# First mixture in pairs of 512 tokens with a written instruction order; second layer of five experts with stationary weights and sums transposed back

## The chip, the cores and the metric

The kernel runs on one core of a Trainium2 chip. The metric is the device time of one launch in microseconds (us), as the median of several runs. TensorE does matmuls and transposes, VectorE, ScalarE and GpSimd do element-wise work, SyncE (SP) issues most DMAs. Instructions of one engine run in the order in which they were issued to it and wait for other engines by semaphores. SBUF is the on-chip memory, PSUM the small memory (eight banks of 128 x 512 fp32) into which TensorE writes.

## The reference

Three layers follow each other: a decayed linear attention over 1536 tokens (2 x 768) of width 512, a first mixture with a cosine as its nonlinearity, and a second mixture in which every token goes to the one of eight experts with the largest gate.

```python
# attention in blocks of 64, with a decayed state; its output is x [1536, 512]
h = x @ w_in                    # [1536, 2048]
x = (h * np.cos(h)) @ w_out     # [1536, 512]

logits = x @ w_gate             # [1536, 8]
e_idx = np.argmax(logits, axis=1)
gate_w = probs[np.arange(N), e_idx]
eom = 1.0 / (1.0 + np.exp(-(x @ w_output_gate)))
for e in range(8):
    mask = e_idx == e
    h = np.maximum(x[mask] @ w1[e], 0.0)            # [., 1024]
    out[mask] = gate_w[mask, None] * eom[mask, e, None] * (h @ w2[e])
```

## The kernel before

All large products are made of three matmuls on fp32 values that are split into a high part (rounded to the fp32r format) and a low part (the rest): high x high, high x low, low x high. `w_in` and `w_out` come as 64-bit floats and are put together from two 32-bit words ("words": a ScalarE operation, three on VectorE, then the high part on ScalarE and the low one on GpSimd). The experts' weights are fp32: the high part is a ScalarE cast (1024 columns, L769 or L203), the low one a VectorE subtraction (L776 or L204).

The tokens of the first mixture are in six blocks `j` of 256, its 2048 hidden columns in eight pieces `p` of 256. One step `("B", j, p)` does one piece for one block. `mm_l1` (L460) makes 24 matmuls with 128 x 128 weights stationary and 256 tokens moving (L467). `chain_parts` (L501) computes h*cos(h) in seven operations that alternate between ScalarE and VectorE (L507, L508, L509, L512, L513, L516, L517), over 512 columns: two halves of the piece by 256 tokens. `mm_l2` (L484) makes 12 matmuls with 128 tokens of the result stationary and 512 columns of `w_out` moving (L488). The second layer of a step is issued two steps behind its first layer (LAG), so that TensorE has other work while the chain runs. Two PSUM banks hold first-layer results; a bank is free when the chain's product (L513) has read it.

The order of steps: six steps (blocks 0 to 2, pieces 0 and 1) run beside the attention; then 24 steps, for each piece the blocks 3, 4 and 5; then 18 steps, blocks 0, 1 and 2 one after the other, pieces 2 to 7. Until the attention ends the instructions stand in an order written out by hand; the steps after it are put in order by a scheduler, with hints (`late`), and from the end of the first mixture on the order is written out again.

When a block is done, the router's pieces follow: `r_evac` adds up its rows, `r_tr` transposes them, `r_mm` multiplies with the gates, `r_arg` picks the expert, `r_rank` (L624) finds each token's place and scatters its row into a table in DRAM by an indirect DMA of GpSimd (L646). Blocks 3, 4 and 5 end first, then 0, 1 and 2. After block 0 the first 128 rows of experts 0 and 1 are read back (`h_rows`, L718) and transposed (`h_prep`, L725).

Experts 0 and 1 are done in two halves of 128 rows (`h_l1`, `h_turn`, `h_l2`), the first before all tokens are routed. Experts 2 to 7 take 208 rows each at once, in four quarters of the hidden columns. For one quarter `c_first` (L779) makes, for each half, four pairs of matmuls with 128 x 128 weights stationary and the tokens moving: 416 columns (high and low parts of the 208 tokens, L477) and 208 columns (L478), then adds the two column groups (L787, L788), applies the relu and splits again. `c_second` (L811) calls `mm_l2`: 12 matmuls with 104 tokens stationary and 512 output columns moving, into two PSUM banks (L488). After the fourth quarter `c_store` scales the rows and scatters them to the output (L699, L701, L702). PSUM is two banks for first layers and six for everything else.

Of the kernel before, what the change touches and what calls it, by code (L numbers as in the profile page):

```python
# [24 lines left out]
WIDE = 256.0  # L25
# [3 lines left out]
def kernel(  # L29
# [29 lines left out]
    EARLY = 0  # L59
# [19 lines left out]
    tmp_p = ctx.enter_context(tc.tile_pool(name="tmp", bufs=2))  # L79

# [50 lines left out]
    HP = 2  # L131
    steps = [("B", j, p) for j in range(FIRST) for p in range(HP)]
# [5 lines left out]
    order.sort(key=lambda z: min(i for i, y in enumerate(steps) if y[2] == z[1]) + 2 * (z[0] == "out"))  # L138
# [26 lines left out]
    nxt = {"load": 0, "split": 0, "free": 0}  # L165
    pools = {}

    def w_load():
# [8 lines left out]
        if not pools.get("spare") and nxt["free"] and i % 3 == 0:  # L177
            pool, tag = xt_p, "xt"
        if "raw2" in pools and i % 2:
            pool = pools["raw2"]  # L180
        t = pool.tile([128, 1024], I32 if words else F32, tag=tag, name="raw")
# [6 lines left out]
    def w_tile(a, p, name):  # L188
        pool = (wa_p if a else wb_p) if p < HP else pools["w2a" if a else "w2b"]
        return pool.tile([128, 2, 1024], F32R, tag=f"w{p}", name=name)  # L190

    half_done, high_done = [], []

    def split_words():
        i = nxt["split"]
        if i >= len(order):
            return
# [3 lines left out]
        if key[0] in ("w1", "w2"):  # L201
            t = w_tile(key[0] == "w1", place(*key), "w_" + "_".join(str(z) for z in key))
            nc.scalar.copy(out=t[:, 0, :], in_=r)  # L203
            nc.vector.tensor_sub(out=t[:, 1, :], in0=r, in1=t[:, 0, :].bitcast(F32))  # L204
            wt[key] = t
            return
        name, p, f = key
        if f == 0:
# [6 lines left out]
        nc.vector.tensor_scalar(x, x, 3, None, ALU.logical_shift_left)  # L215
        nc.vector.scalar_tensor_tensor(
            out=x, in0=low, scalar=29, in1=x, op0=ALU.logical_shift_right, op1=ALU.bitwise_or)
        nc.vector.scalar_tensor_tensor(
            out=x, in0=high, scalar=-0x80000000, in1=x, op0=ALU.bitwise_and, op1=ALU.bitwise_or)
# [6 lines left out]
        half_done.append((hi, lo, xf))  # L226
# [15 lines left out]

    def w_split():
        split_words()
        split_parts()
        w_load()
# [103 lines left out]
    def xs_tile(slot, name="xs"):  # L350
        return xs_p.tile([128, 2, KD, TB], F32R, tag=f"xs{slot}", name=name)
# [88 lines left out]

    def clear_rows():
# [31 lines left out]

    def mm_rows(key, x, f):
# [17 lines left out]
    heads, ends = [], []  # L492

    def late(i, fn):
        with ExitStack() as order:
            if 0 <= i < len(heads):
                for ins in heads[i]:
                    order.enter_context(tc.issue_after(ins))
            fn()

    def chain_parts(h):  # L501
# [3 lines left out]

        def whole():
            head = nc.scalar.activation(out=t, in_=h, func=AF.Identity, bias=quarter, scale=INV2PI / WIDE)  # L507
            heads.append((head.ins, nc.scalar.activation(out=a, in_=t, func=AF.Identity, bias=magic).ins))  # L508
            nc.vector.scalar_tensor_tensor(out=a, in0=a, scalar=MAGIC, in1=t, op0=ALU.subtract, op1=ALU.subtract)  # L509
# [5 lines left out]
        def parts():  # L515
            high = nc.scalar.copy(out=g[:, 0].rearrange("p f t -> p (f t)"), in_=a)  # L516
            low = nc.vector.tensor_sub(  # L517
                out=g[:, 1].rearrange("p f t -> p (f t)"), in0=a,
                in1=g[:, 0].rearrange("p f t -> p (f t)").bitcast(F32))
            ends.append((high.ins, low.ins))  # L520

        return g, whole, wave, parts

    def cos_chain(h):
        g, *fns = chain_parts(h)
        for fn in fns:
            fn()
        return g


# [22 lines left out]
    def r_evac(j, accs):  # L553
        if j == FIRST:
            xr = xs_tile(0, "xrow").bitcast(F32).rearrange("p s k n -> p (s k n)")[:, 0:2 * ROW].rearrange(
                "p (t n) -> p t n", t=2)
        else:
            xr = pools["xr"].tile([128, 2, ROW], F32, tag="xrow", name="xrow")
        if j in part:
            half = part.pop(j)  # L560
            nxt["free"] += 1
            for t in range(2):
                nc.vector.scalar_tensor_tensor(
                    out=xr[:, t, 0:DM], in0=accs[t], scalar=WIDE ** -2, in1=half[:, t * DM:(t + 1) * DM],
                    op0=ALU.mult, op1=ALU.add)
        else:
            nc.scalar.activation(out=xr[:, 0, 0:DM], in_=accs[0], func=AF.Copy, scale=WIDE ** -2)
            nc.vector.tensor_scalar(xr[:, 1, 0:DM], accs[1], WIDE ** -2, None, ALU.mult)
# [3 lines left out]
        xrow_t[j] = xr  # L572

    def r_tr(j, tiles=(0, 1)):
        xr = xrow_t[j]
        if "x2T" not in lps_t:
            lps_t["x2T"] = xs_p.tile([128, KD, TB], F32, tag="xs2", name="x2T")
        x2T = lps_t["x2T"]
        for t in tiles:
            ps = acc_tile([128, KD, 128], "x2ps")  # L580
            for kk in range(KD):
                nc.tensor.transpose(ps[:, kk, :], xr[:, t, kk * 128:(kk + 1) * 128], ident)
            nc.scalar.copy(out=x2T[:, :, t * 128:(t + 1) * 128], in_=ps)

    def r_mm(j):

        lps = acc_tile([128, 512], "lps")
        for kk in range(KD):
            o = 32 * kk % 128
            nc.tensor.matmul(  # L590
                lps[o:o + 32, 0:TB], lhsT=wgs[:, kk, :], rhs=lps_t["x2T"][:, kk, :],
                start=True, stop=True, skip_group_check=True)
        lt = tmp_p.tile([128, 512], F32, tag="t", name="lt")[:, 0:TB]
        nc.vector.tensor_copy(out=lt, in_=lps[:, 0:TB])
        lg_t[j] = lt
# [3 lines left out]
    def r_arg(j):  # L599
        xr = xrow_t[j]  # L600
        lt = lg_t.pop(j)
        ps = acc_tile([128, 512], "l2ps")
        for t in range(2):
            nc.tensor.transpose(ps[:, t * 128:(t + 1) * 128], lt[:, t * 128:(t + 1) * 128], ident)
        lg = xr[:, :, DM:DM + E]
        nc.vector.tensor_reduce(
            out=xr[:, :, DM:DM + 2 * E],
            in_=ps[:, 0:256].rearrange("p (t k e) -> p t e k", t=2, e=32)[:, :, 0:2 * E],
            op=ALU.add, axis=AX.X)
        mx = pools["rt"].tile([128, 2, 1], F32, tag="mx", name="mx")  # L610
        ex = expert[:, 2 * j:2 * j + 2].unsqueeze(2)
        oh = pools["rt"].tile([128, 2, E], F32, tag="oh", name="oh")
        ohb = pools["rt"].tile([128, 2, E], BF16, tag="ohb", name="ohb")
# [652 lines left out]
```

## Time and profile before

| | |
|---|---|
| median of three runs | 528.23 us (527.96 to 528.28) |
| profiled execution, its own time | 529.07 us |
| its span (first to last instruction) | 527.3 us |
| TensorE busy, matmuls | 517.1 us, 98% of the span |
| VectorE, ScalarE, GpSimd busy | 348.2, 308.7, 93.9 us |
| attention with first steps, about | 0 to 100 us |
| first mixture up to its last second layer, about | to 342 us |
| experts 0 and 1, about | to 400 us |
| experts 2 to 7, about | to 521 us |

The durations of single instructions include their passage through the engine. TensorE starts the next matmul long before the end of the one before, so the distance between starts is what an instruction costs there. A row of the timeline gives the start of a group of like instructions, the time to the end of the last, and their number.

### The profile page before, as it was taken

The numbers are of one execution on the slowest core, as the hardware profiler recorded it, in microseconds if no ns is written. First come the engines' busy times: TensorE is split into PE (matmuls) and PEld (weight loads), VectorE is DVE, ScalarE is ACT, GpSimd is POOL, SyncE is SP. The second block draws the span as 40 slices with busy tenths as digits, with TensorE's granted clock in tenths as the row PEclk, the third lists the DMA queues.
The fourth block names the chain that finished last, engine by engine and source line by source line (L and its number), as shares of the span: only waits on it lengthen the run. The fifth ranks groups of instructions, "written<-read, shape, count | busy, mean of one in ns | idle before, by whom it ended". The sixth has DMA issues, their size and how long they took to land. (4 is left out here: it accounts for less than half of the span.)

```text
span 527.3 us, 9379 instructions
## 1 busy us (share of the span) xinstructions
PE 517.1 (98%) x3644; PEld 454.7 (86%) x3644; DVE 348.2 (66%) x652; ACT 308.7 (59%) x536; POOL 93.9 (18%) x129
## 2 busy tenths in 40 slices
PE   8989999999999999999999999999999999999995
PEld 7889988999899899888988898878888888888883
DVE  5887856887877864345466567753478787777731
ACT  3556655676686765554545566544577675766530
POOL 3364110332332320001021010211000101011011
PEclk9999999999999999999999999999999999999999
DMA  8999931346334383201252264726168878776301
GB/s 196 243 264 287 299 117 41 91 177 212 121 96 142 124 295 117 81 0 43 85 203 81 83 201 164 232 100 206 56 222 281 236 238 253 227 221 209 110 28 35
DMA packets 81939, 84.58 MB, mean 160 GB/s; under 512 B 41468, under 2 KB 61948, under 8 KB 81118
## 3 DMA queue, kind: packets, MB, share of 16 engines
q1 hardware_dynamic: 79646, 77.48, 48.5%
q0 software_dynamic: 2240, 6.42, 3.3%
q8 instruction: 30, 0.49, 0.4%
q14 instruction: 23, 0.19, 0.1%
HBM read 66.70 MB, written 17.65 MB: 160 GB/s over the span
## 5 line engine op out<-in xcount | busy, mean ns | idle before, releaser
L488 PE MATMUL acc<-w_out,g 128*128 128x512 f32 x576 | 140.9, 394 | 0.0
L488 PEld LDWEIGHTS acc<-w_out,g 128*128 128x128 f32 x576 | 105.0, 188 | 22.0 <-issue 1.4
L467 PEld LDWEIGHTS h<-xs,w_in 128*128 128x128 f32 x720 | 89.0, 191 | 2.1 <-DVE a L513 0.2
L467 PE MATMUL h<-xs,w_in 128*128 128x256 f32 x720 | 90.7, 283 | 0.0
L488 PE MATMUL acc<-w_w,g 128*104 128x512 f32 x288 | 70.6, 395 | 0.0
L509 DVE SCALAR_TENSOR_TENSOR a<-a,t 128x512 f32<-128x512 f32 x48 | 36.3, 755 | 46.5 <-ACT a L508 46.5
L776 DVE TENSOR_TENSOR w_w<-raw,w_w 128x1024 fp32r<-128x1024 f32 x50 | 60.6, 1216 | 0.8 <-ACT w_w L769 0.8
L488 PEld LDWEIGHTS acc<-w_w,g 128*104 128x104 f32 x288 | 46.7, 168 | 15.4
L477 PE MATMUL hw<-xs,w_w 128*128 128x416 f32 x192 | 59.0, 367 | 0.0
L467 PE MATMUL h<-xback,w_in 128*128 128x256 f32 x432 | 54.9, 283 | 0.0
L467 PEld LDWEIGHTS h<-xback,w_in 128*128 128x128 f32 x432 | 52.8, 189 | 1.4 <-issue 0.8
L507 ACT ACTIVATE t<-h,quarter 128x512 f32<-128x512 f32 x48 | 32.9, 685 | 34.3 <-PE h L467 34.2
L769 ACT CAST w_w<-raw 128x1024 fp32r<-128x1024 f32 x50 | 52.5, 1056 | 0.0
L478 PE MATMUL hw<-xs,w_w 128*128 128x208 f32 x192 | 49.3, 257 | 0.0
L516 ACT CAST g<-a 128x512 fp32r<-128x512 f32 x48 | 29.7, 620 | 32.0 <-DVE a L513 32.0
L513 DVE TENSOR_TENSOR a<-t,h 128x512 f32<-128x512 f32 x48 | 32.9, 685 | 19.6 <-ACT t L512 19.3
L512 ACT ACTIVATE t<-a 128x512 f32<-128x512 f32 x48 | 30.3, 632 | 25.0 <-DVE a L509 25.0
L702 POOL DMA_INDIRECT out_dram<-y,who x16 | 16.1, 1007 | 150.8 <-ACT y L699 147.4
L517 DVE TENSOR_TENSOR g<-a,g 128x512 fp32r<-128x512 f32 x48 | 33.1, 690 | 13.3 <-ACT g L516 12.6
L787 ACT COPY hsum<-hw 128x208 f32<-128x208 f32 x48 | 15.9, 332 | 38.5 <-PE hw L478 38.5
L478 PEld LDWEIGHTS hw<-xs,w_w 128*128 128x128 f32 x192 | 36.7, 191 | 1.0
L477 PEld LDWEIGHTS hw<-xs,w_w 128*128 128x128 f32 x192 | 36.1, 188 | 1.6
(148 smaller groups left out, 717.2 us busy)
## 6 DMA issues: line engine op xcount, KB each, us to landing
raw<-in_moe_w_dram SPq DMA_DIRECT2D x64, 512.0 KB, 4.4
raw<-in_moe_w_in_dram SPq DMA_DIRECT2D x16, 512.0 KB, 3.8
raw<-in_moe_w_out_dram SPq DMA_DIRECT2D x16, 512.0 KB, 3.5
xs_d<-zrow SPq DMA_DIRECT2D x16, 266.0 KB, 4.2
x_d<-xrow SPq DMA_DIRECT2D x6, 532.0 KB, 3.1
k<-in_k_dram SPq DMA_DIRECT2D x12, 256.0 KB, 5.6
q<-in_q_dram SPq DMA_DIRECT2D x12, 256.0 KB, 5.6
v<-in_v_dram SPq DMA_DIRECT2D x12, 256.0 KB, 5.3
```

Source lines behind the costliest of these rows:

```text
L467: nc.tensor.matmul(h[:, f * n:(f + 1) * n], lhsT=wA(key, ws, kk, f), rhs=x[:, xx, kk, :], start=(z == 0), stop=(z == 3 * KD - 1))
L477: nc.tensor.matmul(h, lhsT=wA(key, 0, kk, f), rhs=x[:, kk], start=(kk == 0), stop=False)
L478: nc.tensor.matmul(h[:, 0, :], lhsT=wA(key, 1, kk, f), rhs=x[:, kk, 0, :], start=False, stop=(kk == KD - 1))
L488: nc.tensor.matmul(accs[t][0:m], lhsT=g[:, gs, f, t * m:(t + 1) * m], rhs=wB(key, ws, f), start=(first and n == 0), stop=(last and n == 5))
L507: head = nc.scalar.activation(out=t, in_=h, func=AF.Identity, bias=quarter, scale=INV2PI / WIDE)
L509: nc.vector.scalar_tensor_tensor(out=a, in0=a, scalar=MAGIC, in1=t, op0=ALU.subtract, op1=ALU.subtract)
L512: nc.scalar.activation(out=t, in_=a, func=AF.Sin, scale=-TWOPI)
L513: nc.vector.tensor_mul(out=a, in0=t, in1=h)
L516: high = nc.scalar.copy(out=g[:, 0].rearrange("p f t -> p (f t)"), in_=a)
L517: low = nc.vector.tensor_sub(out=g[:, 1].rearrange("p f t -> p (f t)"), in0=a, in1=g[:, 0].rearrange("p f t -> p (f t)").bitcast(F32))
L769: nc.scalar.copy(out=t[:, 0, :], in_=r)
L776: nc.vector.tensor_sub(out=t[:, 1, :], in0=r, in1=t[:, 0, :].bitcast(F32))
```

## The change

*First mixture.* Blocks 3 and 4, and later blocks 0 and 1, are done in pairs of 512 tokens. A step `("P", j, (p, f))` does one half `f` of a piece for both blocks: 12 matmuls of the first layer with 512 tokens moving (`mm_duo`), the same chain over 512 columns, and 12 of the second layer for four groups of 128 tokens (`mm_duo2`). Blocks 5 and 2 (`SOLO` and the last) stay single. The number of steps stays 48; of the last 18, twelve are those of the pair 0 and 1, then six of block 2. The operands of a pair lie in one tile (`xs01`, `wa01`). Words are done one in each step; experts' weights from step `TURN` (30) on as they fall due (`turn_of`), one in a step, two in step `LATE` - 1 (41). The steps' instructions on TensorE, VectorE and ScalarE are written out in order: pieces of the chain, of a word, of a conversion, and the router's pieces, cut into a TensorE part and a vector part, in places given by `put(step, place, ...)`. PSUM is now two banks for first layers, four (`acc`) and two (`side`).

*Experts 2 to 6.* The second layer has `w2` stationary (128 x 128) and the tokens moving, again 416 and 208 columns, into four banks, one for each 128 output columns (`c_cols`). After the fourth quarter each bank's two column groups are added (a ScalarE copy and a VectorE addition), and at the third quarter of the next expert eight transposes bring the sums back to rows (`c_turn`), which `c_store` scales and scatters as before. Expert 7 is unchanged.

The core of the diff:

```diff
@@ steps, their order, and when pieces of the experts' weights are due
     steps = [("B", j, p) for j in range(FIRST) for p in range(HP)]
     NSA = len(steps)
-    steps += [("B", j, p) for p in range(NP) for j in range(FIRST, NB)]
-    steps += [("B", j, p) for j in range(FIRST) for p in range(HP, NP)]
+    for p in range(NP):
+        steps += [("P", FIRST, (p, f)) for f in range(2)] + [("B", SOLO, p)]
+    TURN = len(steps)
+    steps += [("P", 0, (p, f)) for p in range(HP, NP) for f in range(2)]
+    LATE = len(steps)
+    steps += [("B", FIRST - 1, p) for p in range(HP, NP)]
     NSB = len(steps)
...
         if at < HP:
-            return NSB - (FIRST - 1) * REST if w == "w2" else NSB - (FIRST - 1 - at) * REST
-        return NSB - (NP - at) + (2 if w == "w2" else 0)
+            return TURN + 2 + 5 * at if w == "w2" else LATE - 1
+        return NSB - (NP - at) + (3 if w == "w2" else 0)
@@ the pairs' matmuls
+    def mm_duo(key, x, f):
+        h = pools["l1"].tile([128, 2, TB], F32, tag="l1", name="h")
+        z = 0
+        for kk in range(KD):
+            for ws, xx in ((0, 0), (0, 1), (1, 0)):
+                nc.tensor.matmul(
+                    h, lhsT=wA(key, ws, kk, f), rhs=x[:, :, xx, kk, :], start=(z == 0), stop=(z == 3 * KD - 1))
+                z += 1
+        return h.rearrange("p j t -> p (j t)")
+
+    def mm_duo2(key, g, f, accs, first, last):
+        gf = g.rearrange("p s f t -> p s (f t)")
+        for t in range(4):
+            for n, (gs, ws) in enumerate(((0, 0), (0, 1), (1, 0))):
+                nc.tensor.matmul(
+                    accs[t], lhsT=gf[:, gs, t * 128:(t + 1) * 128], rhs=wB(key, ws, f),
+                    start=(first and n == 0), stop=(last and n == 2))
@@ the experts' second layer
+    def c_cols(e, p, g):
...
+        for z, acc in enumerate(acc_t[e]):
+            cols = slice(z * 128, (z + 1) * 128)
+            for f in range(2):
+                nc.tensor.matmul(
+                    acc, lhsT=wB(("w2", e, p), 0, f)[:, cols], rhs=g[:, :, f, :], start=(p == 0 and f == 0), stop=False)
+                nc.tensor.matmul(
+                    acc[:, 0, :], lhsT=wB(("w2", e, p), 1, f)[:, cols], rhs=g[:, 0, f, :], start=False,
+                    stop=(p == EP - 1 and f == 1))
+            if p == EP - 1:
+                yT = yT_t[e][z // 2][:, z % 2 * LIM:(z % 2 + 1) * LIM]
+                nc.scalar.copy(out=yT, in_=acc[:, 1, :])
+                nc.vector.tensor_add(out=yT, in0=acc[:, 0, :], in1=yT)
...
+    def c_turn(e):
+        yT = yT_t.pop(e)
+        accs = [side_tile([128, KD, 128], "yps") for _ in range(2)]
+        for t in range(2):
+            for z in range(KD):
+                o = z % 2 * LIM + t * HL
+                nc.tensor.transpose(accs[t][0:HL, z, :], yT[z // 2][:, o:o + HL], ident)
+        c_store(e, [a.rearrange("p k n -> p (k n)") for a in accs])
@@ reload of blocks 0 to 2, PSUM, first loads after the attention
+        if (j, p) in ((SOLO, HP - 1), (SOLO, NP - 1)):
+            for z in range(HP) if p == HP - 1 else range(HP, FIRST):
+                t = xs_tile(1) if z >= HP else xpair[0][:, z]
                 nc.sync.dma_start(out=t.bitcast(F32), in_=x_d[z])
...
-    pools["acc"] = ctx.enter_context(tc.tile_pool(name="ps_acc", bufs=6, space=PSUM))
+    pools["acc"] = ctx.enter_context(tc.tile_pool(name="ps_acc", bufs=4, space=PSUM))
+    pools["side"] = ctx.enter_context(tc.tile_pool(name="ps_side", bufs=2, space=PSUM))
...
+    for z in range(4):
+        if z % 2 == 0:
+            t = pools[("w2a", "w2b")[z // 2]].tile([128, 2, 1024], I32, tag=f"w{NP - 1}", name="spot")
+        spot[nxt["load"] + z] = t[:, z % 2]
@@ the written order
+    put(LATE + 1, 4, piece, evac, 0, 0)
...
+    put(LATE + 3, 3, piece, r_arg, 0, 1)
+    put(LATE + 3, 5, piece, r_rank, 0, 0)
+    put(LATE + 3, 6, piece, r_rank, 0, 1)
+    put(LATE + 3, 6, h_rows, 0)
...
+    def step(i):
+        word, pending[:] = pending[:], []
+        chain = first(i)
+        do(i, 1)
+        if i - LAG >= NSA and i not in (LATE + 2, LATE + 3):
+            second(i - LAG)
+        do(i, 2)
+        chain[0]()
+        if word:
+            word[0]()
+        do(i, 3)
+        chain[1]()
+        if word:
+            word[1]()
+        n = 0
+        while n < MOST.get(i, 1) and ripe(i):
+            c_high()
+            n += 1
+        do(i, 4)
+        chain[2]()
+        if nxt["split"] < wide:
+            pending[:] = word_parts()
+        if word:
+            word[2]()
+        do(i, 5)
+        chain[3]()
+        if word:
+            split_parts()
+            w_fill()
+        do(i, 6)
+        for _ in range(n):
+            c_low()
...
     second(NSB - 2)
+    h_prep(0, 0)
+    second(NSB - 1)
     h_l1(H, 0)
-    second(NSB - 1)
...
     for i in range(WHOLE + 2, len(steps) + LAG):
+        e, p = divmod(i - WHOLE, EP)
+        e += HALVED
         if i < len(steps):
             c_first(i, True)
+        if p == 2 and HALVED < e:
+            c_turn(e - 1)
         c_second(i - 2)
+        if p == 2:
+            c_split(e + 1, 1)
```

## Rows read from the trace of the kernel before

**Rows 1.** The page: busy time of each engine, and the granted clock in 40 slices.

```profile
PE 517.1 (98%) x3644; PEld 454.7 (86%) x3644; DVE 348.2 (66%) x652; ACT 308.7 (59%) x536; POOL 93.9 (18%) x129
...
PEclk9999999999999999999999999999999999999999
```

**Rows 2.** Windows: busy time of each engine in four stretches.

```profile
core 0: us, PE busy (x) PEld busy (x) DVE busy (x) ACT busy (x) POOL busy (x), PEclk, DMA share, GB/s
128.00:224.00 96.00, 96.00 (x616) 87.35 (x615) 63.42 (x96) 63.24 (x102) 20.30 (x17) 1.00 0.42 140
224.00:338.00 114.00, 114.00 (x781) 100.89 (x780) 70.00 (x160) 66.38 (x100) 11.32 (x24) 1.00 0.33 113
338.00:380.00 42.00, 41.75 (x220) 33.79 (x219) 17.83 (x61) 17.38 (x38) 6.72 (x6) 1.00 0.43 138
400.00:485.50 85.50, 85.50 (x482) 73.56 (x481) 64.80 (x116) 55.12 (x112) 7.84 (x8) 1.00 0.76 235
```

**Rows 3.** Waits of TensorE's weight loads from 128 us on (in all, times, longest).

```profile
PEld acc L488 <- issue: 1.2, 3, 0.4
PEld h L467 <- issue: 0.8, 2, 0.4
...
PEld h L467 <- DVE a L513: 0.2, 1, 0.2
```

**Rows 4.** Timeline of TensorE, three steps of the first mixture (start, us).

```profile
117.33 2.99 PE L467 MATMUL h<-xs,w_in 128*128 128x256 f32 x24
120.15 2.91 PE L488 MATMUL acc<-w_out,g 128*128 128x512 f32 x12
122.90 3.04 PE L467 MATMUL h<-xs,w_in 128*128 128x256 f32 x24
...
134.14 3.04 PE L467 MATMUL h<-xs,w_in 128*128 128x256 f32 x24
```

**Rows 5.** Timeline of TensorE, one quarter of a whole expert.

```profile
425.53 0.35 PE L477 MATMUL hw<-xs,w_w 128*128 128x416 f32 x1
425.72 0.26 PE L478 MATMUL hw<-xs,w_w 128*128 128x208 f32 x1
...
427.92 2.93 PE L488 MATMUL acc<-w_w,g 128*104 128x512 f32 x12
430.68 0.35 PE L477 MATMUL hw<-xs,w_w 128*128 128x416 f32 x1
```

**Rows 6.** Timeline of TensorE at transposes, and the group of one of them (busy, mean ns).

```profile
344.00 1.04 PE L582 MATMUL x2ps<-ident,xrow 128*128 128x128 f32 x8
344.79 1.64 PE L841 MATMUL hh<-w_w,xs 128*128 128x512 f32 x6
...
422.38 0.52 PE L725 MATMUL xps<-ident,rows 104*128 104x104 f32 x4
422.68 3.01 PE L488 MATMUL acc<-w_w,g 128*104 128x512 f32 x12
...
L582 PE MATMUL x2ps<-ident,xrow 128*128 128x128 f32 x48 | 6.2, 273 | 0.0
```

**Rows 7.** Groups of instructions (busy us, mean ns, idle before): sums of columns, early conversions.

```profile
L788 DVE TENSOR_TENSOR hsum<-hw,hsum 128x208 f32<-128x208 f32 x48 | 17.7, 371 | 25.4 <-ACT hsum L787 24.9
L204 DVE TENSOR_TENSOR w_w<-raw,w_w 128x1024 fp32r<-128x1024 f32 x14 | 17.1, 1222 | 3.8 <-ACT w_w L203 3.8
L787 ACT COPY hsum<-hw 128x208 f32<-128x208 f32 x48 | 15.9, 332 | 38.5 <-PE hw L478 38.5
```

**Rows 8.** Timeline of VectorE and ScalarE, the chain in steps with words.

```profile
142.35 1.27 DVE L509 SCALAR_TENSOR_TENSOR a<-a,t 128x512 f32<-128x512 f32 x1 [1.31 <-ACT a L508]
...
151.43 0.68 ACT L507 ACTIVATE t<-h,quarter 128x512 f32<-128x512 f32 x1
...
152.90 0.69 DVE L509 SCALAR_TENSOR_TENSOR a<-a,t 128x512 f32<-128x512 f32 x1 [1.25 <-ACT a L508]
...
156.42 0.68 ACT L507 ACTIVATE t<-h,quarter 128x512 f32<-128x512 f32 x1
```

**Rows 9.** Timeline of block 0's rows, from their places to their reading, and the landing.

```profile
302.00 0.16 DVE L643 TENSOR_SCALAR ov<-rank 128x2 f32<-128x2 f32 x1
302.20 0.16 DVE L644 TENSOR_TENSOR si<-sl,ov 128x2 int32<-128x2 f32 x1
...
307.41 0.81 SPq L718 DMA_DIRECT2D hrows<-xs_d  x2
...
DMA to landing us min/median/max: 2.7/3.6/4.1
```

More of the change, by code (lines that the diff above doesn't have):

```diff
@@ L490, in mm_l2 @@
                     start=(first and n == 0), stop=(last and n == 5))
[L492 to L499, printed above, removed]
+    ends = []
     def chain_parts(h):
@@ L585, in r_mm, with gates @@
     def r_mm(j):
[L587 to L595, printed above, removed]
+        lps = []
+        def gates():
+            lps.append(side_tile([128, 512], "lps"))
+            for kk in range(KD):
+                o = 32 * kk % 128
+                nc.tensor.matmul(
+                    lps[0][o:o + 32, 0:TB], lhsT=wgs[:, kk, :], rhs=lps_t["x2T"][:, kk, :],
+                    start=True, stop=True, skip_group_check=True)
@@ L597, with kept @@
+        def kept():
+            lt = tmp_p.tile([128, 512], F32, tag="t", name="lt")[:, 0:TB]
+            nc.vector.tensor_copy(out=lt, in_=lps[0][:, 0:TB])
+            lg_t[j] = lt
+        return [gates, kept]
     oh_t = {}
     def r_arg(j):
[L600 to L613, printed above, removed]
-        nc.vector.tensor_reduce(out=mx, in_=lg, op=ALU.max, axis=AX.X)
@@ L653, in r_skip @@
[L653 to L662 removed]
+        got = []
@@ L903 @@
     g_t, y_t, acc_t = {}, {}, {}
[L904 to L921 removed]
+    xpair = {FIRST: xs01, 0: wa01.rearrange("p j s (k t) -> p j s k t", k=KD)}
@@ L967 @@
-    todo = 0
-    def seconds(n):
-        nonlocal todo
-        while todo < n:
-            second(todo)
-            todo += 1
-    def step(i):
-        nonlocal todo
-        turn()
-        if i == NSB - 1:
-            h_prep(0, 0)
-        first(i)
-        turn()
-        seconds(i - LAG + 1)
-        if NSB - FIRST * REST <= i:
-            n = 0
-            while n < 2 and (wide <= nxt["split"] < wide + 2 * EP * HALVED) and turn_of(*order[nxt["split"]]) <= i:
-                late(i - 1, w_split)
-                n += 1
+        if ph == "P":
+            p, f = p
+            head, tail = f == 0 and p == (0 if j == FIRST else HP), f == 1 and p == NP - 1
+            if head:
+                acc_t[j] = [acc_tile([128, DM], "acc") for _ in range(4)]
+            mm_duo2(("out", p), g_t.pop(i), f, acc_t[j], head, tail)
+            return
@@ L1066 @@
     phase.__enter__()
-    ends.clear()
-    heads.clear()
-    assert not rout and todo == NSB - 2
-    H, last = NSB, FIRST - 1
+    w_fill()
     def convert(n=1):
@@ L1082 @@
+    for i in range(NSA + 1, NSB):
+        step(i)
+    ends.clear()
+    H = NSB
     second(NSB - 2)
+    h_prep(0, 0)
+    second(NSB - 1)
     h_l1(H, 0)
-    second(NSB - 1)
-    rout.clear()
+    piece(evac, last, 0)
+    piece(evac, last, 1)
     h_l1(H, 1)
-    r_tr(last, (0,))
-    r_tr(last, (1,))
+    for n in (0, 2, 1, 3):
+        piece(r_tr, last, n)
+    convert_early(1)
     h_l1(H + 1, 0)
+    whole(r_mm(last))
     h_prep(1, 0)
-    r_mm(last)
+    h_l1(H + 1, 1)
+    whole(r_arg(last))
@@ L1092 @@
     h_turn(H)
-    h_l1(H + 1, 1)
-    r_arg(last)
     h_l1(H + 2, 0)
-    r_rank(last)
+    whole(r_rank(last))
     convert_early(1)
```

424 lines of the change are left out of this document (251 added, 173 removed).

## Prediction

> **What bounds the kernel now.** I read the page's busy shares and clock line first [rows 1]: TensorE is busy 98% of the span, VectorE 66%, ScalarE 59%, and the granted clock stays at its upper level, 2.4 GHz, in every slice. The chain that ended last is mostly "issue", so it names no wait to remove. The stretches [rows 2] then show that TensorE does not rest between the end of the attention and the last rows: 96.00 of 96.00 us from 128 to 224, 85.50 of 85.50 from 400 to 485.5, while VectorE there is at 63.42 and 64.80. Weight loads from 128 us on wait for almost nothing [rows 3]. So time is made of TensorE instructions placed one behind the other, and what an edit is worth is read from the distance between starts, not from the duration of one (a matmul of 512 columns lasts 390 ns or so but the next starts long before its end). Two such distances carry the sum. In the first mixture [rows 4] three steps take 134.14 - 117.33 = 16.81 us, 5.60 each: 12 matmuls of 512 columns take 122.90 - 120.15 = 2.75, so the 24 of 256 take 2.85. In a whole expert's quarter [rows 5] the first layer (8 matmuls of 416 and 8 of 208 columns) takes 427.92 - 425.53 = 2.39 and the second (12 of 512) 430.68 - 427.92 = 2.76.
>
> **The change, part by part.**
>
> *Pairs.* 28 steps (16 of the blocks 3 and 4, 12 of the blocks 0 and 1; one of them still beside the attention) issue 12 matmuls of 512 columns in the first layer in place of 24 of 256. The second layer keeps 12 of 512. By [rows 4] a first layer falls from 2.85 to 2.75, so 28 x 0.10 = 2.8 us less. The moving operand now lies in two runs of 256 words; no row shows that form. If each run cost what a matmul of its own does, the gain is nothing; that is the lower bound. I take 2.8, because all the 512-column forms shown, with several operands, agree.
> Rule and row differ here: the rows give 2.85 us for 24 starts, 119 ns each. The Trainium skill ("TensorE: Matmul & The Clock Gate", Back-to-back issue gap) gives columns/2.4 GHz plus 2.5 ns, estimated 2.62 against 2.59 us, so 0.9 us for all pairs. By its figures the experts' part below would give 20 x (2.59 - 2.12) = 9.4. I keep the rows; none of the numbers below uses these two.
>
> *Second layer of experts 2 to 6.* Per quarter 12 matmuls of 512 columns go, and 8 of 416 with 8 of 208 come: the first layer's own list, so its 2.39 us. 20 quarters x (2.76 - 2.39) = 7.4 us less. Each expert then needs eight fp32 transposes. Eight in a row held the engine from 344.00 to the next start at 344.79 [rows 6], 0.79 us; five experts make 4.0. From below four of a smaller form hold it from 422.38 to 422.68, 0.30, which gives 3.0; from above a block that ends before anything else starts takes its whole 1.04, which gives 5.2. I take 4.0: the second layer follows with operands long ready. Net 3.4 less (2.2 to 4.4).
>
> Those transposes wait for the sums in SBUF, and behind them on TensorE stands the next expert's second layer, whose four PSUM banks are freed by the same evacuation. Per expert it is four ScalarE copies at 332 ns and four VectorE adds at 371 ns [rows 7], 1.3 and 1.5 us. They start with the first of four column blocks, each a quarter of 2.39 us, and the next first layer (2.39 us) stands ahead of the transposes: that is the cover. Without it a turn would wait up to 1.5 us. Four experts lie in the 85.5 us window [rows 2]: VectorE 16.2 us and ScalarE 13.8 per expert. They become 17.7 and 15.1 of a period of (85.5 / 4) - 0.7 = 20.7 us. It still fits, so I price the wait at 0, with 5 x 1.0 as its upper bound.
>
> *The written order.* In the stretch with weight words, VectorE and ScalarE now do one word in every step in place of five in four steps; the same 32 words. ScalarE's first operation of a step starts 4.99 us after that of the step before, with one word between [rows 8]; TensorE's new step is 5.50. So it fits, with 0.5 us to spare. The written order puts the first word operation ahead of the subtraction of MAGIC, the second beside the sine and the third beside the cast, so no word operation should lie on the chain. When VectorE's operation met GpSimd it took 1.27 instead of 0.69 [rows 8], 5.57 a step, still only 0.07 over. I price it at 0.
>
> *Moved work.* The four loads into the seventh weight tiles, the earlier reload of blocks 0 and 1, and the 16 clearing stores lie in SP's queue beside loads that wait for a buffer anyway; DMA is at 0.33 to 0.42 there [rows 2], price 0, and a load that came late would show as a ScalarE wait for raw. The router's pieces of blocks 3 to 5 come as TensorE, then vector pieces a step apart; I followed them step by step with the durations shown, and each is ready when TensorE reaches it. Blocks 0 and 1 now end together, only six steps before the end of the mixture. Two things get late by that.
>
> First, the rows of the first experts. From the end of step 45's first layer VectorE needs the chain, 4.99, and 13 small operations 0.2 apart, 2.6. From there the old trace needs 302.20 to 307.41 until SP issues both loads (0.81), and a median of 3.6 to land [rows 9]: 9.6. Together 17.2 us. TensorE reaches the transposes of these rows after 2.75 + 0.79 + 5.60 + 5.60 + 2.75 = 17.5, plus the gate matmuls. Behind them stand the mixture's last second layer and the halved experts. That is tight, with nothing lost if all runs as here.
>
> Second, conversions. Before, 14 pieces of the first two experts' weights were converted before the written end [rows 7]; by the new due steps ten are (one in each of steps 32, 37 and 42 to 47, two in 41). Four times 1.22 us of VectorE move among the router's last small operations, on which TensorE waits. VectorE is busy 17.83 of 42 us there [rows 2], so most fits. I take one conversion that stands in the way, 1.3 us with its handover; bounds 0 and 4 x 1.22 = 4.9.
>
> *Sum.* -2.8 - 3.4 + 1.3 = -4.9 us. The profiled execution took 529.07 us around a span of 527.3, so 524.2 around 522.4; it lies 0.84 above the median of the runs, 528.23, which becomes 523.3.
>
> **The rivals.**
>
> *The vector chain becomes the bound (slower).* Place: the 24 steps from 7 on that still do words. TensorE needs 5.50, and 4.9 us of gain over 24 steps are 0.20: from a cycle of 5.70 on, the kernel is slower. If a contended operation (+0.58) and the sign operation ahead of the low part (+0.4 or so) both come in every step, the cycle is 5.97, the loss 24 x 0.47 = 11.3, the time 534.6. For it: TensorE's load once waited for VectorE's product in this stretch [rows 3]. Against: 4.99 with a word, shown.
>
> *The first experts' rows come a step late.* 5.6 less the margin, then 3.5 to 5 us lost: 526.8 to 528.3. For it: the margin of a few tenths. Against: SP and GpSimd have little else there.
>
> *The turning back waits.* VectorE is then at 86%; if every turn waits 1.0 us, five give back 5 us: 528.3, no change that shows.
>
> *The pairs do not do what they say:* two runs cost two matmuls. Without their 2.8 us, 526.1.
>
> *The transposes cost their whole duration.* One lasts 273 ns [rows 6]; 40 of them one after the other are 10.9 us, not 4.0: 530.2, slower. The block of eight in 0.79 us speaks against it. The Trainium skill ("TensorE: Matmul & The Clock Gate", Part 4: PE-mode transpose) gives about 275 ns in a kernel's context; the trace agrees for one, not for one in a row of eight.
>
> **How the numbers follow.** Forecast 0.60; vector chain 0.09; rows late 0.10; turning waits 0.10; pairs 0.08; transposes 0.03. The forecast's own range is 521.5 to 525.5. From the bounds: all gains and no loss are 528.23 - 2.8 - 4.4 = 521.0; the other cases but two reach 528.3. I give 521.3 to 528.8, which leaves out the chain, the transposes and a little below. About 0.2% (1.06 us) is what a measurement of this kernel tells from no change. Faster by more: the forecast, the pairs, and most of the late rows, 0.60 + 0.07 + 0.06 = 0.73; the same: 0.11, mostly the waiting turns; slower: 0.16.
>
> **What would show it.** Right: first-layer blocks of 12 matmuls 2.75 us apart from the second layer, steps of 5.50 from 106 us to the end of the pairs; a quarter of 4.8 in experts 2 to 6 and a period of 20.7 between their scattered outputs, from 21.4; blocks of eight transposes of 0.8 without idle time before them. Wrong: 512-column starts over 235 ns in the new first layer; TensorE waiting for the product in steps 7 to 30, for the sums before a turn, or for the first experts' rows at the end of the mixture; a granted clock that falls behind such a wait, which would lengthen everything after it.

## The result, and the profile after

The changed kernel takes 522.6 us (median of four runs, 522.28 to 523.34) against 528.16 (527.96 to 528.28): a ratio of 0.9898, 95% interval 0.9882 to 0.9914. That is 5.6 us less. The forecast was 523.3, a gain of 4.9. The profiled execution took 523.34 us around a span of 521.6, so its stretches can be set beside those of before (529.07 and 527.3): 5.7 us less in both.

The page's busy line and clock line, as [rows 1] before:

```profile
PE 511.3 (98%) x3428; PEld 448.9 (86%) x3428; DVE 346.7 (66%) x672; ACT 317.3 (61%) x556; POOL 101.2 (19%) x129
...
PEclk9999999999999999999999999999999999999998
```

TensorE has 216 instructions fewer and is busy 5.8 us less, the whole gain; its share stays at 98% and its granted clock at the upper level, but for a little in the last slice. Next to nothing that waited has been removed. The same four windows as [rows 2], with the same columns:

```profile
128.00:224.00 96.00, 96.00 (x493) 82.30 (x492) 62.15 (x103) 65.98 (x103) 26.32 (x20) 1.00 0.35 110
224.00:338.00 114.00, 113.95 (x638) 93.50 (x637) 67.72 (x158) 63.72 (x96) 15.84 (x20) 1.00 0.39 133
338.00:380.00 42.00, 42.00 (x222) 34.26 (x221) 23.11 (x65) 22.53 (x43) 5.37 (x5) 1.00 0.58 187
400.00:485.50 85.50, 85.50 (x594) 85.10 (x593) 70.24 (x135) 60.04 (x129) 7.92 (x8) 1.00 0.78 240
```

TensorE is without a gap in three and 0.05 us short of it in the other. From 338 to 380 VectorE has gone from 17.83 to 23.11 us and ScalarE from 17.38 to 22.53: those are the conversions that the prediction saw arriving there, and TensorE does not wait for them.

TensorE's timeline in the first mixture, to be read like [rows 4] (start, us, to the end of the last of a group):

```profile
122.88 2.88 PE L511 MATMUL h<-xs,w_in 128*128 128x512 f32 x12
125.60 2.88 PE L520 MATMUL acc<-w_out,g 128*128 128x512 f32 x12
128.32 2.88 PE L511 MATMUL h<-xs,w_in 128*128 128x512 f32 x12
131.04 2.88 PE L538 MATMUL acc<-w_out,g 128*128 128x512 f32 x12
133.76 3.04 PE L499 MATMUL h<-xs,w_in 128*128 128x256 f32 x24
136.63 2.91 PE L520 MATMUL acc<-w_out,g 128*128 128x512 f32 x12
```

A pair's first layer lasts 125.60 - 122.88 = 2.72 us from start to start, 227 ns a matmul; that of the single block keeps 2.87. The two runs of 256 words cost nothing that shows. A pair's step is 5.44 when it follows a pair, and three steps (two of a pair, one of the single block) take 16.50, so 5.50 each, as forecast. The next timeline is of one expert, at its turn, to be read like [rows 5]:

```profile
457.17 0.37 PE L527 MATMUL hw<-xs,w_w 128*128 128x416 f32 x1
...
459.57 1.03 PE L923 MATMUL yps<-ident,yT 128*104 128x128 f32 x8
460.36 0.43 PE L904 MATMUL acc<-g,w_w 128*128 128x416 f32 x1
...
462.84 0.52 PE L803 MATMUL xps<-ident,rows 104*128 104x104 f32 x4
```

The first layer takes 459.57 - 457.17 = 2.40 us, the turn 0.79, and the second layer behind it 462.84 - 460.36 = 2.48. The turn shows no idle time before it. The turn before stands at 438.74, so the period is 20.83 us.

Where the 5.7 us came from, by the starts of the same TensorE work in the two traces:

| up to | before | after | gained so far |
|---|---|---|---|
| end of the first mixture's last second layer (before it is at 342.61, less the 1.44 us of the halved experts that stood ahead of it) | 341.17 | 338.46 | 2.7 |
| first matmul of expert 2 | 387.54 | 384.40 | 3.1 |
| last 36 matmuls, of expert 7 | 512.65 | 506.93 | 5.7 |

```profile
506.93 8.46 PE L538 MATMUL acc<-w_w,g 128*104 128x512 f32 x36
```

```profile
512.65 8.46 PE L488 MATMUL acc<-w_w,g 128*104 128x512 f32 x36
```

These two rows are the same block of TensorE's timeline, after and before. All of the gain has been made when it starts.

### The profile page after: what moved, and what is told of

It reads as the page before. It is cut to its first block, busy times and chain, and to the rows that moved or that the text cites. A ratio compares the mean times of both kernels' runs of the same rounds, so it can differ in the third digit from the quotient of the medians.

```text
span 521.6 us, 8979 instructions
## 1 busy us (share of the span) xinstructions
PE 511.3 (98%) x3428; PEld 448.9 (86%) x3428; DVE 346.7 (66%) x672; ACT 317.3 (61%) x556; POOL 101.2 (19%) x129
## 5 line engine op out<-in xcount | busy, mean ns | idle before, releaser
L854 DVE TENSOR_TENSOR w_w<-raw,w_w 128x1024 fp32r<-128x1024 f32 x55 | 66.7, 1217 | 6.8 <-ACT w_w L847 6.7
L904 PE MATMUL acc<-g,w_w 128*128 128x416 f32 x160 | 50.0, 371 | 0.0
L527 PE MATMUL hw<-xs,w_w 128*128 128x416 f32 x144 | 44.7, 369 | 0.0
L906 PE MATMUL acc<-g,w_w 128*128 128x208 f32 x160 | 41.3, 258 | 0.0
L528 PE MATMUL hw<-xs,w_w 128*128 128x208 f32 x144 | 37.2, 258 | 0.0
L499 PEld LDWEIGHTS h<-xs,w_in 128*128 128x128 f32 x288 | 35.9, 191 | 1.1 <-issue 0.4
L499 PE MATMUL h<-xs,w_in 128*128 128x256 f32 x288 | 36.7, 284 | 0.0
L551 ACT ACTIVATE a<-t,magic 128x512 f32<-128x512 f32 x48 | 34.8, 725 | 1.6
L511 PE MATMUL h<-wa,w_in 128*128 128x512 f32 x144 | 35.2, 393 | 0.0
L268 POOL TENSOR_TENSOR w_out<-x,w_out 128x512 fp32r<-128x512 f32 x16 | 23.7, 1481 | 57.5 <-ACT w_out L262 56.8
```

The source lines that it names most:

```text
L499: nc.tensor.matmul(h[:, f * n:(f + 1) * n], lhsT=wA(key, ws, kk, f), rhs=x[:, xx, kk, :], start=(z == 0), stop=(z == 3 * KD - 1))
L511: nc.tensor.matmul(h, lhsT=wA(key, ws, kk, f), rhs=x[:, :, xx, kk, :], start=(z == 0), stop=(z == 3 * KD - 1))
L527: nc.tensor.matmul(h, lhsT=wA(key, 0, kk, f), rhs=x[:, kk], start=(kk == 0), stop=False)
L528: nc.tensor.matmul(h[:, 0, :], lhsT=wA(key, 1, kk, f), rhs=x[:, kk, 0, :], start=False, stop=(kk == KD - 1))
L904: nc.tensor.matmul(acc, lhsT=wB(("w2", e, p), 0, f)[:, cols], rhs=g[:, :, f, :], start=(p == 0 and f == 0), stop=False)
L906: nc.tensor.matmul(acc[:, 0, :], lhsT=wB(("w2", e, p), 1, f)[:, cols], rhs=g[:, 0, f, :], start=False, stop=(p == EP - 1 and f == 1))
```

## The experiments

Theory: a gain is the sum of TensorE's start distances, and everything else is covered. The rivals: one of the parts gives nothing; the chain, the turns, the first experts' rows or the conversions hold TensorE up. Except where the text says so, each kernel is the changed one with the edit shown; each ratio is against the kernel before, run beside it. Beside these kernels the kernel before had medians of 528.23 to 528.45 where it had 528.16 beside the changed one, so a difference between two medians is good to some 0.3 us. No experiment leaves out a part of the computation.

**The pairs undone.** The pair's first layer as 24 matmuls of 256 columns, all else kept.

```diff
-        z = 0
-        for kk in range(KD):
...
-                    h, lhsT=wA(key, ws, kk, f), rhs=x[:, :, xx, kk, :], ...
+        for jj in range(2):
+            z = 0
+            for kk in range(KD):
...
+                    h[:, jj, :], lhsT=wA(key, ws, kk, f), rhs=x[:, jj, xx, kk, :], ...
```

> The changed kernel, but each pair step makes its first layer with 24 matmuls of 256 columns, one block after the other, in place of 12 of 512; order, chain, second layer and all else stay. Theory (time is the list of TensorE's instructions): 28 x 0.10 = 2.8 us more than the changed kernel, 525.4 us, the first-layer blocks of a step 2.85 us long again. Rival (the written order gives the gain of the first mixture by taking waits away, the pairs little, 0.9 us by the bare issue gap): 522.6 to 523.5.

Measured: 525.93 us (525.81 to 526.79), ratio 0.9958 [0.9945, 0.9972]; 3.3 us over the changed kernel. Its timeline of TensorE:

```profile
121.88 3.04 PE L512 MATMUL h<-xs,w_in 128*128 128x256 f32 x24
124.75 2.91 PE L522 MATMUL acc<-w_out,g 128*128 128x512 f32 x12
127.50 3.04 PE L512 MATMUL h<-xs,w_in 128*128 128x256 f32 x24
...
331.58 5.63 PE L540 MATMUL acc<-w_out,g 128*128 128x512 f32 x24
337.72 0.63 PE L805 MATMUL xps<-ident,hrows 128*128 128x128 f32 x4 [0.52 <-DMA hrows<-xs_d]
```

The first layer takes 2.87 instead of 2.72 us, and the second layer behind it 2.75 instead of 2.72: 0.18 a step for the twelve pair steps from 122.88 us on. For the other sixteen the steps differ by 0.02 to 0.05, since there the 24 matmuls took 2.83 and the 12 mostly 2.76 to 2.80. By the starts that is 12 x 0.18 + 12 x 0.053 + 4 x 0.02 = 2.9 us, and not all of the 3.3. The last row shows a part of the rest: this kernel's TensorE stands still for the first experts' rows, and from 331.58 to its next block at 340.96 it needs 9.38 us where the changed kernel needs 8.69 (329.77 to 338.46). So the pairs do what they say, and they are worth about 2.9.

**The experts' second layer undone.** Experts 2 to 6 with tokens stationary again, and no turn.

```diff
-        if e < E - 1:
-            c_cols(e, p, g_t.pop(i))
-            return
...
-        if p == 2 and HALVED < e:
-            c_turn(e - 1)
```

> The changed kernel, but experts 2 to 6 make their second layer as before: the tokens stationary, 12 matmuls of 512 columns a quarter, no turning back. Theory: the 7.4 us of the matmuls come back and the 40 transposes go; the traces' quarter and transposes gave 2.5 to 3.4 us, so 525.1 to 526.0. Rival (the turning back's waits or the transposes' 273 ns eat what the matmuls gain): within 0.5 us of the changed kernel, or below it.

Measured: 525.21 us (524.96 to 525.34), ratio 0.9937 [0.9924, 0.9949]; 2.6 us over the changed kernel, where the prediction had 3.4. In the traces the stretch from expert 2's first matmul to expert 7's last 36 takes 508.89 - 383.70 = 125.19 us here and 506.93 - 384.40 = 122.53 in the changed kernel, 2.66 less.

**Both undone**, so that only the order, the tiles and the queues are new.

> Both undone: the first layer of the pairs in matmuls of 256 columns, the experts' second layer with tokens stationary. What is left of the change is the written order, the pairing of the steps and the division of PSUM. Theory: the two parts add, 522.6 + 2.8 + 2.5 = 527.9, so the order alone is worth about 0.3 us against the kernel before. Rival (the order takes waits away): 526 or less. Rival (the order costs and the parts give more than their sum): over 529.

Measured: 528.77 us (528.16 to 529.8, twelve runs), ratio 1.0008 [0.9999, 1.0017], which takes in 1. The order alone gains nothing, and costs 0.9 us at most by that interval. This kernel's TensorE also waits for the first experts' rows, 0.26 us. The parts add up: by the medians -3.3 - 2.6 + 0.4 = -5.5, by the starts -2.9 - 2.7 = -5.6, against 5.6 measured.

**High products first.** In both layers of experts 2 to 6 all matmuls of 416 columns ahead of those of 208, so that one form follows itself (the loop over the forms is taken outside).

> The changed kernel; in the whole experts' first layer the four matmuls with the weights' high part (416 columns) come first and the four with the low part (208 columns) after them, and in the turned second layer the two of 416 before the two of 208, in place of alternating. The trace has 206 ns from a 416 start to the next and 95 from a 208 start, 301 a pair. Theory that each start costs its columns and some 12 to 17 ns, as at 256 (119) and 512 (227): 187 and 99, 15 ns a pair less; 8 pairs in 24 first layers and 20 second ones make 5.3 us less, 517.3. Rival (a start waits for the weights' own load, so a short matmul cannot hide the next load): 190 and 110, no change, 522.6.

Measured: 522.54 us (522.44 to 522.7), the same. Its timeline of one quarter:

```profile
420.45 1.00 PE L527 MATMUL hw<-xs,w_w 128*128 128x416 f32 x4
421.29 0.60 PE L529 MATMUL hw<-xs,w_w 128*128 128x208 f32 x4
421.72 0.94 PE L527 MATMUL hw<-xs,w_w 128*128 128x416 f32 x4
422.49 0.59 PE L529 MATMUL hw<-xs,w_w 128*128 128x208 f32 x4
```

Four of 416 and four of 208 take 421.72 - 420.45 = 1.27 us with the end of a transposition in it and 422.92 - 421.72 = 1.20 without, which is half of the 2.40 above. The split has moved, the sum has not: alternating, the distance is about 206 ns behind a start of 416 columns and 95 behind one of 208; grouped, about 190 and 106. That is what the rival forecast, in which a start waits for its weights' load. TensorE's weight loads are busy 85.10 of 85.50 us from 400 us on in the changed kernel, where before it was 73.56, but no run separates the loads from the columns. A price for one form, read from a mixed list, holds for that list only.

**Each transpose of the turn twice.**

```diff
-                nc.tensor.transpose(accs[t][0:HL, z, :], ...)
+                for _ in range(2):
+                    nc.tensor.transpose(accs[t][0:HL, z, :], ...)
```

> The changed kernel with each of the eight transposes of a turn issued twice, the second into the same place. Theory (a turn holds TensorE for 0.79 us and nothing hides it): 5 x 0.79 to 0.87 = 4.0 to 4.4 us more, 526.6 to 527.0. Rival (a turn mostly waits for the sums, so more transposes hide in nothing or cost their 273 ns each): 522.6, or 533.5.

Measured: 526.99 us (526.57 to 528.37, twelve runs), 4.4 over the changed kernel: 0.88 for eight transposes, not 0.79, and far from the 8 x 273 = 2.2 us that their durations would give. Its turns on TensorE's timeline:

```profile
438.88 1.91 PE L924 MATMUL yps<-ident,yT 128*104 128x128 f32 x16
...
460.58 1.91 PE L924 MATMUL yps<-ident,yT 128*104 128x128 f32 x16
```

The period is 21.70 where it was 20.83, 0.87 more: eight starts 109 ns apart.

**A longer chain of word operations.** One, two and three additional VectorE operations (a shift by nothing, 0.42 us each) in each of the 24 words done after the attention:

```diff
+            if "side" in pools:
+                for _ in range(3):
+                    nc.vector.tensor_scalar(x, x, 0, None, ALU.logical_shift_left)
```

> The changed kernel with one more VectorE operation (a shift by 0 over 512 words, about 0.42 us) in the middle of each word after the attention, 24 of them, ahead of the chain's product. Theory (TensorE's step of 5.47 us covers a vector chain of about 4.9): chain 5.35, no change, 522.6. Rival (the chain is already the bound of these steps): 24 x 0.42 = 10 us more, 532.6.

> The changed kernel with two more VectorE operations in each word after the attention. One more cost nothing; with three the chain's first operations stood 6.00 us apart in place of TensorE's 5.47. Theory (a chain of 4.74 us and 0.42 for each operation, so 5.58): 23 x 0.11 = 2.5 us more, 525.2, with starts 5.58 apart. Rival (TensorE's step still covers it): 522.6.

> The same with three such operations in each word: chain about 6.2 us against TensorE's 5.47. Theory: the chain becomes the bound, 24 x 0.7 = 17 us more, 539, with TensorE waiting for the product (its weight loads for a first-layer bank). If the chain had a whole step of slack that is never used up: 522.6.

Measured: with one 522.73 us (522.37 to 523.02), with two 526.34 (525.83 to 526.65), with three 534.97 (534.13 to 536.0): 0.1, 3.7 and 12.4 over the changed kernel. First ScalarE's timeline of the changed kernel, at the operation that begins a chain:

```profile
153.33 0.69 ACT L550 ACTIVATE t<-h,quarter 128x512 f32<-128x512 f32 x1 [0.78 <-PE h L499]
...
158.80 0.69 ACT L550 ACTIVATE t<-h,quarter 128x512 f32<-128x512 f32 x1 [0.65 <-PE h L511]
...
164.24 0.69 ACT L550 ACTIVATE t<-h,quarter 128x512 f32<-128x512 f32 x1 [0.62 <-PE h L511]
```

Then the same with three operations more:

```profile
148.13 0.68 ACT L553 ACTIVATE t<-h,quarter 128x512 f32<-128x512 f32 x1
...
154.14 0.68 ACT L553 ACTIVATE t<-h,quarter 128x512 f32<-128x512 f32 x1
```

and the waits of TensorE's weight loads in that kernel (in all, times, longest):

```profile
PEld h L514 <- DVE a L561: 6.3, 10, 0.7
PEld h L502 <- DVE a L561: 4.0, 6, 0.7
PEld h L514 <- ACT w_in L265: 1.8, 1, 1.8
...
PEld h L514 <- POOL w_in L271: 1.3, 1, 1.3
```

In the changed kernel the chain waits for TensorE in each step, 0.62 to 0.78 us; its turns are TensorE's steps, 5.50 on average. With three more operations the chain does not wait, its turns are 6.0 apart, and TensorE waits for the product. So the chain with a word is 6.0 - 3 x 0.42 = 4.74 long and its cover about 0.7. One more operation (5.16) must be free and is.

With two, the expectation spread the loss over 23 steps. The trace shows it in one place. The chain's turns are 5.55 there, yet TensorE takes 88.00 us from 111.15 to 199.15, as the changed kernel does from 111.76 to 199.76. Then comes the last piece's `w_in`:

```profile
202.02 2.91 PE L523 MATMUL acc<-w_out,g 128*128 128x512 f32 x12
205.81 0.73 PE L514 MATMUL h<-xs,w_in 128*128 128x512 f32 x2 [0.88 <-ACT w_in L265]
207.41 4.11 PE L514 MATMUL h<-xs,w_in 128*128 128x512 f32 x10 [0.87 <-POOL w_in L271]
```

```profile
208.00:212.00 4.00, 4.00 (x12) 3.17 (x11) 3.59 (x7) 2.80 (x5) 0.64 (x1) 0.57 0.10 26
```

TensorE waits for the word's high part and then for its low part, and behind these waits the granted clock is 0.57 for four us: for most of them it is the lower level, 1.2 GHz. The ten matmuls take 3.91 us to the next start, at 211.32, where at 227 ns they take 2.27. From 199.15 to 214.16 this kernel needs 15.01 us, the changed one 11.06 (199.76 to 210.82): 3.95, the whole loss. The written order does one word in a turn of the chain. In the changed kernel the chain makes up what it lags behind the attention, by turns of 4.71 to 4.83 from 100.84 to 115.18 us; with two operations more it never does, and the words come late with it.

With three, 16 steps take 96.00 us in place of 88.00, so TensorE loses 8.0 to the product, and 4.55 at the same last word (15.61 from 207.09 to 222.70 in place of 11.06): 12.55, and 12.4 came. The expectation for three, 17 us, took a chain of 6.2, and that word was in no expectation. In the changed kernel neither the chain nor the words are the bound; from the second operation on they cost time, and with two it is a word that comes late, not the product.

**The first experts' rows.** One kernel puts the read of these rows a step later in the written order, one lets TensorE want them a second layer (12 matmuls, 2.8 us) earlier:

```diff
-    put(LATE + 3, 6, h_rows, 0)
+    put(LATE + 4, 6, h_rows, 0)
```

```diff
-    second(NSB - 2)
     h_prep(0, 0)
+    second(NSB - 2)
     second(NSB - 1)
```

> The changed kernel with the reading of the first experts' first rows issued one step later (step 46 in place of 45). The trace of the changed kernel has the read issued at 331.86 us and its transposes at 335.25 without a wait. Theory (the margin is used up): the read goes out behind step 46's own vector work, 5 to 6 us later, and TensorE waits that long before the transposes: 527 to 529 us. Rival (some steps of slack behind it, other work of TensorE fills it): 522.6.

> The changed kernel with the transposes of the first experts' first rows one second layer earlier on TensorE (ahead of step 46's, 2.75 us). The place of the read in the written order has turned out not to set its time; the scatter's landing does. Theory (the read is issued at 331.86 us and lands in 3.1 to 3.9, so the rows are there only tenths before 335.25): TensorE waits 2.4 to 2.8 us, 525.0 to 525.4. Rival (the rows are there long before): 522.6.

Measured: 522.92 us (522.39 to 524.13), no change, and 525.22 (524.8 to 526.38), 2.6 over the changed kernel. First the changed kernel's timelines of GpSimd, SP and TensorE, to be read like [rows 9]:

```profile
325.87 0.97 POOL L712 DMA_INDIRECT xs_d<-xrow,si  x1 [0.30 <-issue]
...
331.98 0.10 POOL L610 MEMSET xrow<- 128x8 f32 x1 [5.14 <-DMA xs_d<-xrow,si]
...
331.86 0.81 SPq L796 DMA_DIRECT2D hrows<-xs_d  x2
...
326.81 3.12 PE L499 MATMUL h<-xs,w_in 128*128 128x256 f32 x24
329.77 5.64 PE L538 MATMUL acc<-w_out,g 128*128 128x512 f32 x24
335.25 0.60 PE L803 MATMUL xps<-ident,hrows 128*128 128x128 f32 x4
```

With the read put a step later:

```profile
325.00 0.98 POOL L712 DMA_INDIRECT xs_d<-xrow,si  x1 [0.30 <-issue]
...
330.83 0.81 SPq L796 DMA_DIRECT2D hrows<-xs_d  x2
```

With the rows wanted earlier, TensorE's timeline:

```profile
325.95 3.12 PE L499 MATMUL h<-xs,w_in 128*128 128x256 f32 x24
...
333.96 0.63 PE L803 MATMUL xps<-ident,hrows 128*128 128x128 f32 x4 [2.14 <-DMA hrows<-xs_d]
```

SP's read waits until the scatter has landed, 5.99 us behind the last scatter's issue in the one, 5.83 in the other; GpSimd waits 5.14 us for the same landing. Its place in the list does not set its time, so the first kernel could not test what it was made for, and "a step late costs 3.5 to 5 us" fell for this edit. The second kernel gives the margin: there the rows are used at 333.96, and that execution runs 326.81 - 325.95 = 0.86 ahead, so in the changed kernel they are there at 334.82, 0.43 us before TensorE comes to them at 335.25. Tight, and nothing lost. In the two kernels with the pairs undone the read went out 7.13 and 7.11 us behind the last scatter's issue, and there TensorE waited 0.52 and 0.26 us; why the scatter landed later in these two, no run shows.

**More pieces converted in the mixture.** `w2` pieces due one step earlier, and two pieces a step in the mixture's last four steps:

```diff
-        return NSB - (NP - at) + (3 if w == "w2" else 0)
+        return NSB - (NP - at) + (2 if w == "w2" else 0)
-    MOST = {LATE - 1: 2}
+    MOST = {i: 2 for i in (LATE - 1, NSB - 4, NSB - 3, NSB - 2, NSB - 1)}
```

> The changed kernel with more of the first two experts' weights due before the end of the mixture: the pieces of the second layer one step earlier, and up to two conversions in each of the last four steps, as near to the 14 of the kernel before as the loads allow. Theory after the result (the moved conversions are hidden, since TensorE never rests from 338 to 380 us): no change, 522.6 within 0.3. Rival (the prediction's 1.3 us are there and something else gives more): 521.3 or so.

Measured: 544.87 us (543.29 to 545.21), ratio 1.0304 [1.0281, 1.0327]; 22 us slower, which neither theory had. Its waits from 290 to 400 us (in all, times, longest), its window from 300 to 380, and a row of ScalarE's timeline:

```profile
PEld acc L538 <- ACT g L561: 10.9, 2, 9.4
ACT w_w L847 <- DMA raw<-in_moe_w_dram: 10.8, 3, 5.9
```

```profile
300.00:380.00 80.00, 62.99 (x366) 52.01 (x365) 41.82 (x98) 34.12 (x50) 8.85 (x9) 0.91 0.46 154
```

```profile
312.23 1.99 ACT L847 CAST w_w<-raw 128x1024 fp32r<-128x1024 f32 x2 [2.16 <-PE acc L538]
```

The pieces now stand in the order before their tile is free (2.16 us for TensorE's second layer) or their data is there (10.8 us in all, 5.9 at the longest). ScalarE waits, the chain's cast stands behind it, and TensorE waits for that cast (10.9 us); it is busy 62.99 of 80 us at a granted clock of 0.91. So this kernel tells what badly placed conversions cost, not which of its two edits does it, and nothing of whether those behind the mixture are hidden.

**The conversions behind the mixture, doubled.** The VectorE subtraction of the six pieces done early there is issued twice:

```diff
-                convert()
+                c_high()
+                t, r, _ = low_due[0]
+                nc.vector.tensor_sub(out=t[:, 1, :], in0=r, in1=t[:, 0, :].bitcast(F32))
+                c_low()
```

> The changed kernel with VectorE's subtraction (1.22 us) issued twice in each of the six conversions of the first two experts' weights that now stand behind the mixture's last step, 7.3 us more of VectorE among the router's last operations. Theory (they are hidden, TensorE does not rest there; one of six may stand in the way): 522.6 to 523.2. Rival (the prediction's price, 1.3 us of TensorE for 4.9 us of VectorE): about 1.9 us more, 524.5.

Measured: 528.67 us (526.91 to 528.87, twelve runs), ratio 0.9997 [0.9988, 1.0005]: 6.1 over the changed kernel. The profiled run, 527.25, is one of the shorter ones and 4.7 over; what the longer ones add is in no trace. The window behind the mixture and the waits of TensorE's loads:

```profile
338.00:361.00 23.00, 20.99 (x116) 16.23 (x115) 17.70 (x35) 12.38 (x17) 2.85 (x3) 1.00 0.56 185
```

```profile
PEld acc L982 <- ACT hg L971: 2.1, 1, 2.1
PEld hh L955 <- DVE w_w L854: 1.8, 1, 1.8
PEld l2ps L658 <- DVE lt L644: 1.1, 1, 1.1
```

VectorE is at 77% there and still TensorE's loads wait 5.0 us, for the logits' copy, for a weight and for a split result: 7.3 us of additional VectorE work are not covered. In the changed kernel these three waits are absent, so as they stand the conversions are hidden, with little to spare. The theory that they are hidden held for the six pieces and fell for twice six.

## Why the prediction was right, point by point

**The bound.** Right: time is TensorE's starts, and the gain is what the starts lost. The clock, the shares and the absence of waits are as forecast.

**Pairs, -2.8.** Right: 2.9 by the starts, and 3.3 by the medians, which hold a wait for the first experts' rows. That the number came so near is in part luck. The term took one price, 0.10, for all 28 steps; twelve gave 0.18 and sixteen 0.02 to 0.05. Its 2.85 was the mean of blocks of 2.82 and 2.87 in [rows 4], and its 2.75 came from a kernel in which every second layer follows a first layer of 24; behind a first layer of 12 both are 2.72. The rule of the Trainium skill that was weighed ("TensorE: Matmul & The Clock Gate", Back-to-back issue gap), which the section gives for an isolated matmul, would give 0.9 for this part, an estimate; the trace does not agree: 119 to 120 ns at 256 columns, 227 to 231 at 512.

**Experts' second layer, -3.4.** Right in kind, 2.6 measured. Two terms were a little off. A quarter came to 2.41, not 2.39: 20 x (2.76 - 2.41) = 7.0, not 7.4. A turn came to 0.87, not 0.79, because the block behind a transposition takes 0.08 longer too (2.48 instead of 2.40): 5 x 0.87 = 4.35, not 4.0. 7.0 - 4.35 = 2.65, and 2.66 is what the stretches of the two traces differ by. The distance to the next start, from which the price of eight transposes was read, holds only part of their price. That the turns wait, the rival, is ruled out: no idle time stands before a turn. That they cost their whole duration is ruled out by the doubling.

**Written order, words at 0.** Right. The margin forecast as 0.5 is about 0.7, and the slower rival stayed away. With two additional operations a word it comes, first as a late word, with three as a late product too.

**First experts' rows.** Right, and as narrow as said: 0.3 forecast, 0.43 found, and in two of the kernels the rows came too late. The price of the rival, 3.5 to 5 us, was not met there: TensorE waited for what was missing, 0.52 and 0.26.

**Conversions, +1.3.** This term was too high. TensorE waits for no conversion; between 338 and 380 us it is busy 42.00 of 42 us where before it was 41.75, since a wait of 0.25 us for VectorE in the router is gone. The order as a whole cost 0.4 us in its own run (up to 0.9 by the interval), which again holds a wait for the first experts' rows. The two doubled and misplaced sets of conversions show that the fear was not idle: 4.7 to 6.1 us for 7.3 us of VectorE, 22 us for pieces placed too early.

So the sum, -4.9, met -5.6 with errors that partly cancel: 0.1 too little gain for the pairs, 0.75 too much for the experts, and 1.3 of loss that did not come. The pairs and the experts have each a run of their own that settles them. That the conversions cost nothing rests on the trace and on the doubled ones, as the run that was to move them did not test it. No run gave a version faster than the changed kernel beyond what can be told apart. What stays open is why a 512-column start with `wa01` as the operand takes 231 ns and with `xs01` 227, and why the scatter landed later in two kernels.

## What to carry to other kernels

Where TensorE has no gap, cost an edit by the distance between starts in a block of the same form, and count the block behind it as well. A vector chain that is covered shows it in the first operation of each turn: as long as that one waits for TensorE, its wait is the cover, here 0.7 us a step, and one can spend it but not twice. What is made beside the chain has its own due time: here it was a word, not the product, that came late first. A written order is only as good as its waits: an instruction placed before its buffer is free or its data has landed holds up whatever stands behind it on its engine, while one that waits for a transfer anyway can be placed late for nothing.

## What the runs showed of the hardware that was not expected

- Eight fp32 transposes of 128 columns start 109 ns apart, though each lasts 272 ns, and the block of matmuls behind them takes 0.08 us longer.
- Matmuls of 416 and 208 columns cost about 301 ns a pair in an alternating list (206 and 95) and the same in a grouped one (190 and 106).
- A read of a DRAM table that an indirect scatter has written was issued 5.8 to 6.0 us after the last scatter's issue in the changed kernel and the two made for these rows, a step later in the order or not, and 7.1 us in the two kernels with the pairs undone.
- With two additional word operations two waits of TensorE of 0.88 and 0.87 us, 0.7 us apart, were followed by four us at a granted clock of 0.57, and ten matmuls of 512 columns took 3.91 us in place of 2.27. In the kernel with the rows wanted earlier one wait of 2.14 us was followed by a granted clock of 1.00.
